# Sigmoid attention and a Swish feed-forward layer in one kernel: loading the first head group in halves, doubling the last value tile on chip, and reordering the products

## The chip, the cores and the metric

The kernel runs on one core of a Trainium2 chip. The metric is the device time of one execution in microseconds.

## What is computed

```python
# q, k, v: (8, 12, 448, 64): batch, heads, sequence, head size
scores = q @ k.T / sqrt(64) - log(448)
attn   = 1 / (1 + exp(-scores))             # a sigmoid, no row sums
x      = (attn @ v) -> (3584, 768)          # tokens x (heads * head size)
h      = x @ w_in                           # 768 x 2048
g      = h / (1 + exp(-beta * h))           # beta: one number per column
out    = g @ w_out                          # 2048 x 768, float32
```

## The kernel before, in words

Matmul operands are fp16, sums are fp32. The 12 heads of a batch are taken four at a time, a *group* g (24 groups, three per batch), and a group has two *slots* of two heads. `load_one` (L111) brings q and k of a group to the chip from POOL's queue, with a cast; `transpose` on DVE makes `qT` and `kT` (L183, L191, L195) in blocks of 32. `load_v` loads a batch's values. The 448 keys are three tiles of 128 and a last one of 64 keys; for odd slots the last tile is needed on partitions 64 to 127, so `load_v_last` loads it twice, with four loads (L144), for the lower and for the upper partitions.

`visit(g, jt)` computes the scores of one key tile for both slots on PE (L205) into two score tiles in PSUM, and ACT turns each into attention weights (L216). `attend(g)` multiplies them with the values on PE (L271) into two PSUM banks, and DVE copies these to `xT` (L280). `half_visit` does the same for half the queries (QH = 224) in batch 0's three groups, so that the first layer can begin early. `dense1` is a unit of the first layer: one column tile of 128, six matmuls (L289), a sigmoid on ACT (L297) and a product on DVE (L300) that writes `gt`.

The second layer takes most token tiles in pairs, by Strassen's scheme (`strassen`): seven products i of half size in place of eight, each in two parts of four matmuls (L401), with sums of `gt` on DVE (L390), copies from PSUM to `osb` on ACT for i = 1 and 2 (L423, L425), and additions on DVE (L420). The first three token tiles and the last are done plainly (`dense2`, L319, L332). `store` sends `osb` out from SP's queue (L454).

The order is written by hand (`manual_schedule`): each engine takes its instructions in program order. At the start PE runs matmuls without a use (`idle_units`, L513) while loads arrive. Later, a planner puts units of the list `fill` (first and second layer) between the visits: each visit adds to a budget (`spread`, then `rest`), and units with nominal costs (`M1_US`, `M1H_US`, `M2_US`) are taken until it is spent. Outside the score tiles, PSUM has four banks for everything. `bank` gives the one that has been out of use longest; a Strassen product that stays open is `held`. Ahead of an attend, the planner finishes units while more than one bank is held and the next unit opens one; the third entry that `second_layer` yields says so.

Of the kernel before, what the change touches and what calls it, by code (L numbers as in the profile page):

```python
# [8 lines left out]
FP32 = mybir.dt.float32  # L9
FP16 = mybir.dt.float16  # L10
# [3 lines left out]
def kernel(  # L14
# [10 lines left out]
    nc = tc.nc  # L25
# [26 lines left out]

    const = ctx.enter_context(tc.tile_pool(name="const", bufs=1))
    rawp = ctx.enter_context(tc.tile_pool(name="rawp", bufs=3))
    vp = ctx.enter_context(tc.tile_pool(name="vp", bufs=3))
    qTp = ctx.enter_context(tc.tile_pool(name="qTp", bufs=4))
    kTp = ctx.enter_context(tc.tile_pool(name="kTp", bufs=4))
    attnp = ctx.enter_context(tc.tile_pool(name="attnp", bufs=12))
    xTp = ctx.enter_context(tc.tile_pool(name="xTp", bufs=3))
    sump = ctx.enter_context(tc.tile_pool(name="sump", bufs=3))  # L60
    sigp = ctx.enter_context(tc.tile_pool(name="sigp", bufs=3))
    outp = ctx.enter_context(tc.tile_pool(name="outp", bufs=3))
    psum = {}
    used = {}
    held = {}
# [38 lines left out]
    raws = {}  # L104
    vs = {}

    def load_one(g: int, r: int, c0: int = 0, c1: int = NB):
        b, t = divmod(g, QPB)
        if g not in raws:
            raws[g] = rawp.tile([P, 2, NB, D], FP16, tag="raw", name="raw")  # L110
        nc.gpsimd.dma_start(  # L111
            out=raws[g][:, r, c0:c1].rearrange("p c d -> p (c d)"),
            in_=(q, k)[r][b, HQ * t : HQ * (t + 1)].rearrange("h (p c) d -> (h p) (c d)", c=NB)[
                :, c0 * D : c1 * D
            ],
        )

    def load_qk(g: int):
# [9 lines left out]
    def load_v(b: int):  # L128
        vs[b] = vp.tile([P, H, JF + 1, D], FP16, tag="v16", name="v16")
        rows = v[b].rearrange("h (p c) d -> p h (c d)", c=NB)  # L130
        for i in range(HQ):
            nc.gpsimd.dma_start(  # L132
                out=vs[b][i * BLK : (i + 1) * BLK, :, 0:JF].rearrange("p h j d -> p h (j d)"),
                in_=rows[:, :, JF * i * D : JF * (i + 1) * D],
            )
        if b > 0:
            load_v_last(b)

    def load_v_last(b: int):
        rows = v[b].rearrange("h (p c) d -> p h c d", c=NB)  # L140
        for base in (0, KL):
            for c in range(NF, NB):
                lo = base + (c - NF) * BLK
                nc.gpsimd.dma_start(  # L144
                    out=vs[b][lo : lo + BLK, :, JF], in_=rows[:, :, c]
                )

    WCH = 8
    WOUT = 2
# [24 lines left out]
    def in_order(b: int, t):  # L174
        t = t.rearrange("p c e -> p (c e)").bitcast(FP32)
        return t.rearrange("p (q c) -> p c q", c=NB) if b == B - 1 else t

    def transpose(g: int, r: int, c0: int = 0, c1: int = NB):
        raw = raws[g][:, r]
        if r == 0:  # L180
            if g not in qT:
                qT[g] = qTp.tile([P, NB * BLK, PAIR], FP16, tag="qT", name="qT")
            nc.vector.transpose(  # L183
                out=in_order(g // QPB, qT[g][:, c0 * BLK : c1 * BLK]),
                in_=raw[:, c0:c1].rearrange("p c d -> p (c d)").bitcast(FP32),
            )
            return
        kT[g] = kTp.tile([P, S, PAIR], FP16, tag="kT", name="kT")
        to = kT[g].rearrange("p k e -> p (k e)").bitcast(FP32)
        frm = raw.rearrange("p c d -> p (c d)").bitcast(FP32).rearrange("p (c f) -> p c f", c=NB)  # L190
        nc.vector.transpose(  # L191
            out=to[:, 0 : JF * P].rearrange("p (j i q) -> p i j q", j=JF, i=HQ),
            in_=frm[:, 0:NF].rearrange("p (i j) f -> p i j f", j=JF),
        )
        nc.vector.transpose(  # L195
            out=to[:, JF * P :], in_=frm[:, NF:].rearrange("p c f -> p (c f)")
        )

    def score_tile():
        return psum["sc"].tile([P, 2, 512], FP32, tag="sco", name="sco")  # L200
# [41 lines left out]
    def half_visit(g: int, c0: int, second: int):  # L242
        slots = (2 * g, 2 * g + 1)
        scos = [score_tile() for _ in slots]
        plan = [(s, jt, sco, jt * QH) for jt in (0, 1) for s, sco in zip(slots, scos)]
        widths = [S, S]
        if second:
            plan = [(s, 2, sco, 0) for s, sco in zip(slots, scos)]
            plan += [(s, JF, scos[0], QH) for s in slots]
            widths = [S, QH]  # L250
        for i in range(0, len(plan), 2):
            for e in range(PAIR):
                for s, jt, sco, u0 in plan[i : i + 2]:
                    for hh in range(2):
                        score(sco, u0, s, jt, hh, e, c0, QH)
        ats = {id(sco): weigh(sco, n) for sco, n in zip(scos, widths)}
        for s, jt, sco, u0 in plan:
            at_tiles[s, jt, c0] = ats[id(sco)][:, :, u0 : u0 + QH]
# [133 lines left out]
    def strassen(t: int, i: int, part: int):  # L392
# [29 lines left out]
        if i == 1:  # L422
            nc.scalar.copy(out=o2[:, L], in_=a)  # L423
        elif i == 2:
            nc.scalar.copy(out=o1[:, L], in_=m2)  # L425
            add(o1[:, R], r, o1[:, L])
            release((t, "s"))
        elif i == 3:
            add(o2[:, L], m2, o2[:, L])
            release((t, "b"))  # L430
        elif i == 4:
            add(o2[:, R], a, o2[:, L], ALU.subtract)
        elif i == 5:
            add(o2[:, R], r, o2[:, R])
            release((t, "r"))
            store(t + 1, 0, DM)
        elif i == 6:
            add(o1[:, L], a, o1[:, L], ALU.subtract)
            release((t, "a"))
            store(t, 0, DM)  # L440
# [19 lines left out]
    def second_layer(tiles):  # L460
        for t in tiles:
            if t < 3 or t == NT - 1:
                for half in range(2):
                    for part in range(N2):
                        yield M2_US / N2, lambda a=(t, half, part): dense2(*a), False
            elif t % 2:
                for i in range(NPROD):
                    for part in range(2):
                        yield M2_US / 4, lambda a=(t, i, part): strassen(*a), i in (2, 3)

    def filler_stream():
        for c0 in (0, QH):
# [24 lines left out]
    firsts = ctx.enter_context(ExitStack())  # L497
    share_psum(firsts, 3, 2)
    with tc.manual_schedule():
        load_one(0, 0, 0, NH)  # L500
        load_one(0, 1)
        nc.gpsimd.memset(nlogs, NEG_LOG_S)
        nc.gpsimd.memset(dummy, 0.0)
        nc.scalar.activation(out=dummy, in_=dummy, func=AF.Sigmoid, bias=0.0, scale=1.0)
# [7 lines left out]
            for _ in range(n):  # L512
                nc.tensor.matmul(idle, still[:, 0:P], still, start=True, stop=True)  # L513

        idle_units(13)
        for g in range(1, QPB):
            load_one(g, 0, 0, NH)
            load_one(g, 1)
        load_v(0)
        load_v_last(0)  # L520
        nc.sync.dma_start(out=beta_in[0:NDC], in_=moe_beta.rearrange("(c p) -> c p", p=P))
        for g in range(QPB):
            load_one(g, 0, NH, NB)
        for c in range(WCH):
            load_w_in(c)
        for g in range(QPB):
            transpose(g, 0, 0, NH)
            transpose(g, 1)

        for g in range(QPB):  # L530
            for second in range(2):
                half_visit(g, 0, second)
                if g == QPB - 1:
                    attend(0, 0, QH, (second,))
                if 2 * g + second < 2 * QPB - 1:
                    idle_units(4 if g < QPB - 1 else 2)
        for g in range(QPB):
            transpose(g, 0, NH, NB)
        attend(1, 0, QH, (0,))
        half_visit(0, QH, 0)  # L540
        attend(1, 0, QH, (1,))
        for i in range(P // BLK):
            part = slice(i * BLK, (i + 1) * BLK)
            nc.vector.transpose(out=beta_sb[part], in_=beta_in[:, part])
        attend(2, 0, QH)
        load_qk(3)
        load_w_out(0, 0)
        load_w_out(1, 0)
# [2 lines left out]
        load_qk(5)  # L551
        load_w_out(0, 1)
        load_w_out(1, 1)
        half_visit(0, QH, 1)

        firsts.close()
        share_psum(ctx, 2, 4)
# [5 lines left out]
                fill_units(1 + g)  # L563
        fill_units(2)
        attend(QPB - 1, QH, QH)
        transpose(QPB, 0)
        transpose(QPB, 1)
        fill_units(4)

        visits = [(QPB, jt, ()) for jt in range(JF + 1)]  # L570
        for g in range(QPB + 1, NQUAD, 2):
            visits += [(g, jt, ()) for jt in range(JF)] + [(g, JF, (g + 1,))]
            visits += [(g + 1, jt, ()) for jt in range(JF)]
        spread = [3 * M1H_US] * 2 + [M2_US, 6 * M1H_US] + [5 * M2_US / 7] * 7
        spread += [2.95] * (sum(g < 4 * QPB for g, _, _ in visits) - len(spread))

        total = sum(u[0] for u in fill[at_fill[0] :])
# [13 lines left out]
        for i, (g, jt, also) in enumerate(visits):  # L591
            if jt == 0:
                if g > QPB:

                    while len(held) > 1 and (len(held) > 2 or fill[at_fill[0]][3]):
                        spent += fill[at_fill[0]][0]
                        fill_units(1)
                    attend(g - 1, 0, S)
                if g + 2 < NQUAD:
                    if g + 2 not in raws:  # L600
                        load_qk(g + 2)
                if g + 1 < NQUAD and (g + 1) % QPB == 0:
                    load_v((g + 1) // QPB)
            visit(g, jt, also)
            if jt in (1, 2) and QPB < g < NQUAD - 1:
                transpose(g + 1, jt - 1)
            for name, part in adds.get(i, ()):
                weight_sum(name, part)
            budget += spread[i] if i < len(spread) else rest
            if (g, jt) == (QPB, JF):  # L610
                fill_units(3)
                spent += 3 * M1H_US
                transpose(g + 1, 0)
                transpose(g + 1, 1)
            goal = max(budget, spent + LEAST_US) if g > QPB + 2 else budget
# [38 lines left out]
```

## Time and profile before

| | us |
|---|---|
| median of 3 runs (391.8 to 392.15) | 391.82 |
| the profiled run | 391.83 |
| its span, first to last instruction | 390.1 |
| PE busy | 382.3 |
| ACT busy | 247.2 |
| DVE busy | 219.7 |
| POOL busy | 77.0 |

The profile records when each instruction ran, and what it had waited for. Engines: PE (matmuls; PEld is its weight loads), DVE (vector), ACT (activation functions), POOL and SP (here: issuing loads and stores). A busy PE is not a PE at its peak, because matmuls overlap each other; the distance from one start to the next says how fast they go. L271 is line 271 of the kernel before.

### The profile page before, as it was taken

Reading aid. Unit: us, or ns where it says so; the run is one execution under the profiler, and the core shown is the slowest. Engines: PE = TensorE matmul, PEld = TensorE weight load, DVE = VectorE, ACT = ScalarE, POOL = GpSimd, SP = SyncE. Lnnn points to the kernel's source line nnn. Section 1 sums busy time; section 2 is a strip of 40 time slices with the busy share of each in tenths; the row PEclk is TensorE's granted clock in tenths of the full one; section 3 lists DMA queues with packets and bytes.
Section 4 is the critical chain, followed back from the end, with each engine's and each line's share of the span. In section 5 each row is a group of like instructions: output and inputs, shape, how many; then the busy total and the mean of one; then the engine's idle time right before and its main releaser. Section 6 shows DMA issues by size and latency. Waiting matters only on the chain.

```text
span 390.1 us, 7403 instructions
## 1 busy us (share of the span) xinstructions
PE 382.3 (98%) x2991; PEld 191.4 (49%) x2991; DVE 219.7 (56%) x417; ACT 247.2 (63%) x341; POOL 77.0 (20%) x133
## 2 busy tenths in 40 slices
PE   8999999999999999999999999999999999999996
PEld 3468664444454444444454444544445444555563
DVE  2346364774655556555665556655675555555752
ACT  3987866688474796597465784567863677725200
POOL 7843353232110610150110510114100000000000
PEclk9999999999999999999999999999999999999999
DMA  8999999949252880547353581629113210030033
GB/s 120 158 187 202 185 179 203 208 86 95 49 105 63 125 92 4 119 69 71 49 117 81 83 81 28 126 50 163 27 22 82 52 31 2 1 82 0 2 81 121
DMA packets 48801, 35.08 MB, mean 90 GB/s; under 512 B 28272, under 2 KB 45184, under 8 KB 48768
## 3 DMA queue, kind: packets, MB, share of 16 engines
q0 software_dynamic: 43376, 23.60, 46.5%
q1 hardware_dynamic: 5392, 11.02, 10.5%
q8 instruction: 23, 0.38, 0.4%
q14 instruction: 10, 0.08, 0.1%
HBM read 47.19 MB, written 11.01 MB: 149 GB/s over the span
## 4 chain that ended last, share of the span: by engine, by line
PE 82%; DMA 9%; DVE 3%; POOL 2%; issue 2%; ACT 1%; SPq 0%; DVEq 0%; POOLq 0%
PE m_ps L289 37%; PE m_ps L401 25%; PE sco L205 9%; PE av_ps L271 8%; DMA w_out<-in_moe_w_out_dram 4%; PE m_ps L319 3%; DMA w_in<-in_moe_w_in_dram 2%; DMA out_dram<-osb 2%; DMA v<-in_v_dram 2%; POOL raw L111 1%; DVE osb L420 1%; DVE sum L390 1%; ACT osb L425 0%; POOL v L132 0%; SPq L454 0%
## 5 line engine op out<-in xcount | busy, mean ns | idle before, releaser
L216 ACT ACTIVATE attnT<-sco,nlogs 128x896 f16<-128x896 f32 (+1 forms) x171 | 160.4, 991 | 74.8 <-PE sco L205 74.1
L289 PE MATMUL m_ps<-xT,w_in 128*128 128x448 f16 (+1 forms) x864 | 154.3, 332 | 0.6 <-DMA w_in<-in_moe_w_in_dram 0.6
L300 DVE TENSOR_TENSOR gt<-m_ps,sg 128x448 f16<-128x448 f32 (+1 forms) x144 | 79.7, 571 | 87.2 <-ACT sg L297 87.1
L289 PEld LDWEIGHTS <-w_in 128*128 128x128 f16 x864 | 80.4, 98 | 71.3 <-issue 14.9
L297 ACT ACTIVATE sg<-m_ps,beta_sb 128x448 f32<-128x448 f32 (+1 forms) x144 | 82.1, 595 | 31.2 <-PE m_ps L289 29.8
L401 PEld LDWEIGHTS <-sum 128*128 128x128 f16 x480 | 45.1, 98 | 36.4 <-issue 7.9
L420 DVE TENSOR_TENSOR osb<-m_ps,osb 128x384 f32<-128x384 f32 x60 | 33.3, 555 | 38.4 <-ACT osb L425 19.5
L205 PE MATMUL sco<-qT,kT 32*128 32x448 f16 (+3 forms) x864 | 51.9, 340 | 0.5 <-DVE qT L183 0.2
L401 PE MATMUL m_ps<-w_T,sum 128*128 128x384 f16 x288 | 50.6, 327 | 0.0
L111 POOL DMA_DIRECT2D raw<-in_q_dram x27 | 14.9, 552 | 172.2 <-DVE kT L195 167.7
L271 PE MATMUL av_ps<-attnT,v 128*64 128x448 f16 (+3 forms) x432 | 43.3, 341 | 1.9 <-DVE osb L420 1.9
L280 DVE CAST xT<-av_ps 128x448 f16<-128x448 f32 (+1 forms) x54 | 28.7, 567 | 26.0 <-PE av_ps L271 26.0
L390 DVE TENSOR_TENSOR sum<-gt 128x1024 f16<-128x1024 f16 x60 | 39.0, 678 | 0.1
L401 PE MATMUL m_ps<-w_T,gt 128*128 128x384 f16 x192 | 33.9, 327 | 0.0
L401 PE MATMUL m_ps<-w_out,sum 128*128 128x384 f16 x192 | 33.7, 327 | 0.0
L271 PEld LDWEIGHTS <-v 128*64 128x64 f16 (+1 forms) x432 | 19.3, 108 | 27.3 <-issue 21.5
L205 PEld LDWEIGHTS <-kT 32*128 32x128 f16 (+1 forms) x864 | 13.5, 96 | 28.3 <-issue 26.0
L401 PEld LDWEIGHTS <-gt 128*128 128x128 f16 x192 | 18.1, 98 | 14.8 <-issue 3.1
L319 PE MATMUL m_ps<-w_out,gt 128*128 128x384 f16 (+2 forms) x128 | 22.5, 327 | 0.4 <-DMA w_out<-in_moe_w_out_dram 0.4
L132 POOL DMA_DIRECT2D v<-in_v_dram x32 | 19.8, 631 | 12.9 <-DMA w_out<-in_moe_w_out_dram 6.7
L144 POOL DMA_DIRECT2D v<-in_v_dram x32 | 19.5, 619 | 14.3 <-DMA w_out<-in_moe_w_out_dram 6.9
L183 DVE STREAM_TRANSPOSE qT<-raw 128x448 f32<-128x448 f32 (+1 forms) x27 | 16.4, 614 | 2.8 <-DMA raw<-in_q_dram 2.8
(23 smaller groups left out, 95.5 us busy)
## 6 DMA issues: line engine op xcount, KB each, us to landing
out_dram<-osb SPq DMA_DIRECT2D x98, 96.0 KB, 1.9
raw<-in_k_dram POOLq DMA_DIRECT2D x24, 224.0 KB, 4.9
raw<-in_q_dram POOLq DMA_DIRECT2D x21, 224.0 KB, 3.7
v<-in_v_dram POOLq DMA_DIRECT2D x32, 144.0 KB, 6.6
w_in<-in_moe_w_in_dram POOLq DMA_DIRECT2D x8, 384.0 KB, 11.0
w_out<-in_moe_w_out_dram POOLq DMA_DIRECT2D x4, 768.0 KB, 14.9
v<-in_v_dram POOLq DMA_DIRECT2D x32, 48.0 KB, 5.8
out_dram<-osb SPq DMA_DIRECT2D x2, 384.0 KB, 2.3
```

Source lines behind the costliest of these rows:

```text
L132: nc.gpsimd.dma_start(out=vs[b][i * BLK : (i + 1) * BLK, :, 0:JF].rearrange("p h j d -> p h (j d)"), in_=rows[:, :, JF * i * D : JF * (i + ...
L205: nc.tensor.matmul(sco[base : base + nk, hh, u0 : u0 + n], kT[g][lo : lo + BLK, jt * P : jt * P + nk, e], qT[g][lo : lo + BLK, c0 : c0 + n ...
L216: nc.scalar.activation(out=at[:, :, 0:n], in_=sco[:, :, 0:n], func=AF.Sigmoid, bias=nlogs[:, 0:1], scale=MSCALE,)
L271: nc.tensor.matmul(av[hh * D : (hh + 1) * D, 0:n], vs[b][base : base + nk, 2 * (s % NPAIR) + hh, jt], at[base : base + nk, hh, 0:n], start ...
L280: nc.vector.tensor_copy(out=xTs[b][:, s % NPAIR, c0 : c0 + n], in_=av[:, 0:n])
L289: nc.tensor.matmul(m1[:, 0:n], w_in16[:, hc, dc * P : (dc + 1) * P], xTs[b][:, hc, c0 : c0 + n], start=(hc == 0), stop=(hc == NHC - 1),)
L297: nc.scalar.activation(out=sg[:, 0:n], in_=m1[:, 0:n], func=AF.Sigmoid, bias=0.0, scale=beta_sb[:, dc : dc + 1])
L300: nc.vector.tensor_tensor(out=gt[:, dc, off : off + n], in0=m1[:, 0:n], in1=sg[:, 0:n], op=ALU.mult)
L319: nc.tensor.matmul(m2, gt[:, dc, cols(t)], w_out16[:, dc, lo:hi], start=(dc == 0), stop=(dc == NDC - 1),)
L390: nc.vector.tensor_tensor(out=sums[t, i], in0=x, in1=y, op=op)
L401: nc.tensor.matmul(m2, (x if op is None else sums[t, i])[:, dc], w[:, dc], start=first and dc == 0, stop=(dc == ND - 1), skip_group_check= ...
L420: nc.vector.tensor_tensor(out=out, in0=in0, in1=in1, op=op)
```

## The change

- The first group's q and k come in two pairs of heads, and transposes and scores of the first half visit are ordered by slot. The second half of its queries is loaded ahead of the values.
- The last value tile is loaded once, to the lower partitions. A DVE copy, `double_v_last`, brings it to the upper ones: for batch 0 after its first attend, for batch 1 after the key transposes of group 3, for the others at the third visit of their first group.
- The second query half's scores of group 0 move between the attends of the first half.
- Between `attend(2)` and the planner, five units surround the transposes of group 3 in place of four; the first entries of `spread` change.
- The copy of product i = 2 moves from ACT to DVE; part 0 of product 4 counts as a unit that comes ahead of an attend.
- There are two value buffers for three, four output buffers for three, and 10 idle matmuls at the start for 13.

```diff
-    vp = ctx.enter_context(tc.tile_pool(name="vp", bufs=3))
+    vp = ctx.enter_context(tc.tile_pool(name="vp", bufs=2))
-    outp = ctx.enter_context(tc.tile_pool(name="outp", bufs=3))
+    outp = ctx.enter_context(tc.tile_pool(name="outp", bufs=4))
...
-        if b > 0:
-            load_v_last(b)
-
-    def load_v_last(b: int):
         rows = v[b].rearrange("h (p c) d -> p h c d", c=NB)
-        for base in (0, KL):
-            for c in range(NF, NB):
-                lo = base + (c - NF) * BLK
-                nc.gpsimd.dma_start(
-                    out=vs[b][lo : lo + BLK, :, JF], in_=rows[:, :, c]
-                )
+        for c in range(NF, NB):
+            lo = (c - NF) * BLK
+            nc.gpsimd.dma_start(out=vs[b][lo : lo + BLK, :, JF], in_=rows[:, :, c])
+
+    def double_v_last(b: int):
+        nc.vector.tensor_copy(out=vs[b][KL:P, :, JF], in_=vs[b][0:KL, :, JF])
...
+        if (g, c0) == (0, 0):
+            plan.sort(key=lambda x: x[0])
+            side = 1
...
         elif i == 2:
-            nc.scalar.copy(out=o1[:, L], in_=m2)
+            nc.vector.tensor_copy(out=o1[:, L], in_=m2)
...
-                        yield M2_US / 4, lambda a=(t, i, part): strassen(*a), i in (2, 3)
+                        yield M2_US / 4, lambda a=(t, i, part): strassen(*a), i in (2, 3) or (i, part) == (4, 0)
...
-        load_one(0, 0, 0, NH)
-        load_one(0, 1)
+        for h in (0, 2):
+            load_one(0, 0, 0, NH, h, h + 2)
+            load_one(0, 1, 0, NB, h, h + 2)
...
-        idle_units(13)
+        idle_units(10)
         for g in range(1, QPB):
             load_one(g, 0, 0, NH)
             load_one(g, 1)
+        load_one(0, 0, NH, NB)
         load_v(0)
-        load_v_last(0)
         nc.sync.dma_start(out=beta_in[0:NDC], in_=moe_beta.rearrange("(c p) -> c p", p=P))
-        for g in range(QPB):
+        for g in range(1, QPB):
             load_one(g, 0, NH, NB)
...
                 half_visit(g, 0, second)
-                if g == QPB - 1:
-                    attend(0, 0, QH, (second,))
                 if 2 * g + second < 2 * QPB - 1:
                     idle_units(4 if g < QPB - 1 else 2)
-        for g in range(QPB):
-            transpose(g, 0, NH, NB)
+        attend(0, 0, QH, (0,))
+        double_v_last(0)
+        half_visit(0, QH, 0)
+        attend(0, 0, QH, (1,))
+        for g in range(1, QPB):
+            transpose_q(g, NH, NB)
         attend(1, 0, QH, (0,))
-        half_visit(0, QH, 0)
         attend(1, 0, QH, (1,))
...
-        attend(2, 0, QH)
+        attend(2, 0, QH, (0,))
+        half_visit(0, QH, 1)
+        attend(2, 0, QH, (1,))
         load_qk(3)
         load_w_out(0, 0)
         load_w_out(1, 0)
         load_v(1)
         load_qk(4)
         load_qk(5)
         load_w_out(0, 1)
         load_w_out(1, 1)
-        half_visit(0, QH, 1)
...
         attend(QPB - 1, QH, QH)
+        fill_units(1)
         transpose(QPB, 0)
+        fill_units(2)
         transpose(QPB, 1)
-        fill_units(4)
+        double_v_last(1)
+        fill_units(2)
...
-        spread = [3 * M1H_US] * 2 + [M2_US, 6 * M1H_US] + [5 * M2_US / 7] * 7
+        spread = [4 * M1H_US, M1H_US + M2_US, 6 * M1H_US, 3 * M2_US / 4]
+        spread += [17 * M2_US / 4 / 7] * 7
...
             if jt in (1, 2) and QPB < g < NQUAD - 1:
                 transpose(g + 1, jt - 1)
+            if jt == 2 and g % QPB == 0 and g > QPB:
+                double_v_last(g // QPB)
...
             if (g, jt) == (QPB, JF):
                 fill_units(3)
-                spent += 3 * M1H_US
+                spent += 3 * M2_US / N2
```

More of the change, by code (lines that the diff above doesn't have):

```diff
@@ L105, with load_one @@
     vs = {}
-    def load_one(g: int, r: int, c0: int = 0, c1: int = NB):
+    def load_one(g: int, r: int, c0: int = 0, c1: int = NB, h0: int = 0, h1: int = HQ):
         b, t = divmod(g, QPB)
@@ L111, in load_one @@
         nc.gpsimd.dma_start(
[L112 to L115, printed above, removed]
+            out=raws[g][h0 * BLK : h1 * BLK, r, c0:c1].rearrange("p c d -> p (c d)"),
+            in_=(q, k)[r][b, HQ * t + h0 : HQ * t + h1].rearrange(
+                "h (p c) d -> (h p) (c d)", c=NB
+            )[:, c0 * D : c1 * D],
         )
@@ L176, in in_order, with transpose_q, transpose_k, transpose @@
         return t.rearrange("p (q c) -> p c q", c=NB) if b == B - 1 else t
-    def transpose(g: int, r: int, c0: int = 0, c1: int = NB):
-        raw = raws[g][:, r]
-        if r == 0:
[L181 to L197, printed above, removed]
+    def transpose_q(g: int, c0: int = 0, c1: int = NB, rows=slice(0, P)):
+        if g not in qT:
+            qT[g] = qTp.tile([P, NB * BLK, PAIR], FP16, tag="qT", name="qT")
+        nc.vector.transpose(
+            out=in_order(g // QPB, qT[g][rows, c0 * BLK : c1 * BLK]),
+            in_=raws[g][rows, 0, c0:c1].rearrange("p c d -> p (c d)").bitcast(FP32),
+        )
+    def transpose_k(g: int, last: int, rows=slice(0, P)):
+        if g not in kT:
+            kT[g] = kTp.tile([P, S, PAIR], FP16, tag="kT", name="kT")
+        to = kT[g][rows].rearrange("p k e -> p (k e)").bitcast(FP32)
+        frm = raws[g][rows, 1].rearrange("p c d -> p (c d)").bitcast(FP32)
+        frm = frm.rearrange("p (c f) -> p c f", c=NB)
+        if last:
+            to, frm = to[:, JF * P :], frm[:, NF:].rearrange("p c f -> p (c f)")
+        else:
+            to = to[:, 0 : JF * P].rearrange("p (j i q) -> p i j q", j=JF, i=HQ)
+            frm = frm[:, 0:NF].rearrange("p (i j) f -> p i j f", j=JF)
+        nc.vector.transpose(out=to, in_=frm)
+    def transpose(g: int, r: int):
+        if r == 0:
+            transpose_q(g)
+        else:
+            transpose_k(g, 0)
+            transpose_k(g, 1)
     def score_tile():
@@ L245, in half_visit @@
         plan = [(s, jt, sco, jt * QH) for jt in (0, 1) for s, sco in zip(slots, scos)]
-        widths = [S, S]
+        widths, side = [S, S], 2
+        if (g, c0) == (0, 0):
+            plan.sort(key=lambda x: x[0])
+            side = 1
         if second:
@@ L249, in half_visit @@
             plan += [(s, JF, scos[0], QH) for s in slots]
-            widths = [S, QH]
-        for i in range(0, len(plan), 2):
+            widths, side = [S, QH], 2
+        for i in range(0, len(plan), side):
             for e in range(PAIR):
-                for s, jt, sco, u0 in plan[i : i + 2]:
+                for s, jt, sco, u0 in plan[i : i + side]:
                     for hh in range(2):
@@ L525 @@
             load_w_in(c)
-        for g in range(QPB):
-            transpose(g, 0, 0, NH)
-            transpose(g, 1)
+        halves = (slice(0, KL), slice(KL, P))
+        for rows in halves:
+            transpose_q(0, 0, NH, rows)
+            transpose_k(0, 0, rows)
+        for rows in halves:
+            transpose_k(0, 1, rows)
+        for g in range(1, QPB):
+            transpose_q(g, 0, NH)
+            transpose_k(g, 0)
+            transpose_k(g, 1)
+        transpose_q(0, NH, NB)
         for g in range(QPB):
@@ L532 @@
                 half_visit(g, 0, second)
-                if g == QPB - 1:
-                    attend(0, 0, QH, (second,))
                 if 2 * g + second < 2 * QPB - 1:
                     idle_units(4 if g < QPB - 1 else 2)
-        for g in range(QPB):
-            transpose(g, 0, NH, NB)
+        attend(0, 0, QH, (0,))
+        double_v_last(0)
+        half_visit(0, QH, 0)
+        attend(0, 0, QH, (1,))
+        for g in range(1, QPB):
+            transpose_q(g, NH, NB)
         attend(1, 0, QH, (0,))
-        half_visit(0, QH, 0)
         attend(1, 0, QH, (1,))
```

## The prediction

> **What bounds the kernel now.** I read the page first, then the chain of waits in order of time, then PE's own timeline, and last the landing times of single loads.
>
> ```profile
> span 390.1 us, 7403 instructions
> PE 382.3 (98%) x2991; PEld 191.4 (49%) x2991; DVE 219.7 (56%) x417; ACT 247.2 (63%) x341; POOL 77.0 (20%) x133
> ```
>
> The profiled run took 391.83 us, 1.7 us outside its span, and the median of the runs is 391.82, so I sum in the span and add 1.7. A PE that is busy for 98% leaves gains only where its matmuls start late. The chain says where that is, from the start to 63 us:
>
> ```profile
> 6.52 6.91 DMA v<-in_v_dram
> ...
> 13.71 0.82 POOL w_in L153
> 14.53 7.82 DMA w_in<-in_moe_w_in_dram
> ...
> 49.76 13.65 DMA w_out<-in_moe_w_out_dram
> ```
>
> Up to there one stream of loads, issued by POOL in program order, sets the end; after 63.45 us the chain is nearly all PE. In PE's timeline I compared each group of matmuls with its undisturbed twin, start to start. From 41.94 us on it loses: 0.22 and 0.46 us in the scores of `visit(3,1)` and `visit(3,2)` (0.73 and 0.97 us against 0.51), 0.63 us at the w_out load that lands at 63.4, and at six attends, those that follow Strassen products, 0.43 us five times (2.00 against 1.57) and 0.88 us once, together 3.03. That makes 4.34 us.
>
> **The part that decides.** The change loads the last value tile once and lets DVE copy it to the upper partitions. For batch 1 that copy, `double_v_last(1)`, stands on DVE right after the key transposes of group 3. When does DVE get there, and when has its input landed?
>
> ```profile
> 38.57 0.20 DVE L195 STREAM_TRANSPOSE kT<-raw 128x64 f32<-128x64 f32 x1
> 38.70 0.73 DVE L300 TENSOR_TENSOR gt<-m_ps,sg 128x224 f16<-128x224 f32 x2
> 39.59 0.12 PEld L205 LDWEIGHTS <-kT 32*128 32x128 f16 x8 [0.18 <-DVE gt L300]
> ```
>
> ```profile
> L144 POOL DMA_DIRECT2D v<-in_v_dram x1: 609/609/609, 37.1 to 37.1; - x1
> ...
> DMA to landing us min/median/max: 11.5/11.5/11.5
> ```
>
> DVE ends those transposes at 38.8 us. The two loads that the copy reads are the first two of L144 for batch 1; they are issued at 36.53 and 37.13 and land 11.8 and 11.5 us later, at 48.3 and 48.6, behind two w_out loads of 768 KB. The order of POOL's issues there is unchanged. Before, only `attend(3)` at 52.25 us needed them, so the wait was hidden; now DVE stands at its copy for some 9 us. Queued behind it are the products gt (L300) of the next first-layer units. Each frees one of four PSUM banks, so PE can run four more units and the unit after them, column tile 7 of batch 0's second half, stops it.
>
> Does DVE really let ready work stand?
>
> ```profile
> 103.08 0.48 ACT L425 COPY osb<-m_ps 128x384 f32<-128x384 f32 x1 [0.82 <-PE m_ps L401]
> 103.59 0.56 DVE L420 TENSOR_TENSOR osb<-m_ps,osb 128x384 f32<-128x384 f32 x1 [1.35 <-ACT osb L425]
> 104.06 0.68 DVE L390 TENSOR_TENSOR sum<-gt 128x1024 f16<-128x1024 f16 x1
> 104.27 0.76 PE L271 MATMUL av_ps<-attnT,v 128*64 128x448 f16 x6
> 104.66 0.55 DVE L420 TENSOR_TENSOR osb<-m_ps,osb 128x384 f32<-128x384 f32 x1
> 105.26 1.07 PE L271 MATMUL av_ps<-attnT,v 128*64 128x448 f16 x10 [0.24 <-DVE osb L420]
> ```
>
> Yes: the sum at 104.06 reads only gt, complete long before, and its buffer was free when PE ended the third product at about 103.0; it still ran behind the add that DVE idled 1.35 us for. The Trainium skill, "TensorE: Matmul & The Clock Gate", Part 1, says the same, that VectorE's queue is strict FIFO; if it were not, rival A would be the result.
>
> *When PE goes on.* Loads land earlier than before by two terms. Two 48 KB loads of v(0) fall out; the last two of L144 there landed at 15.0 and 15.3, the one before at 14.5: 0.8 us. And the stream had a dip:
>
> ```profile
> 11.00:14.00 3.00, 3.00 (x38) 1.19 (x38) 0.00 (x0) 3.00 (x4) 2.07 (x5) 1.00 1.88 173
> 14.00:17.00 3.00, 3.00 (x54) 1.38 (x42) 0.60 (x2) 2.95 (x4) 3.00 (x5) 1.00 1.00 124
> ```
>
> At 124 instead of 173 GB/s (last column) 3 us lose 0.85. POOL issued the first w_in load only at 13.71, after a wait for a landing of v; now smaller loads stand ahead of it and it should go out some 2 us sooner. I take 0.7 (0 to 0.85). Landing: 48.6 − 0.8 − 0.7 = 47.1 (46.9 to 47.8). Then the copy, 768 fp16 elements on 64 partitions, a shape not in the trace: the sum of 1024 takes 0.68 us, the smallest transposes 0.20; I take 0.4, nearer to the middle because a copy reads one operand. Then gt, 0.39 us (L300 at 128x224), and 0.1 of waits: PE resumes at 48.0 us (47.5 to 49).
>
> *What is then left of PE's work.* Before, the same work (tiles 0 to 6, `visit(3,0)`) is done at 41.94 us, with 348.1 us still to go. This does not depend on the edits ahead of it: group 0 by head pairs, the earlier query halves, `half_visit(0,QH,·)` among the attends, 10 idle matmuls for 13 all end in the same wait, so I cost them at nothing. Were the wait gone, they would be worth at most the 1.5 us by which w_in lands earlier, because PE already waits for w_in at 22.4.
>
> *Clock.* PE stands idle from about 40.5 (41.94 less up to 1.5) to 48.0, for 7.5 us. What a PE does after standing still, the start of the span shows:
>
> ```profile
> 1.19 5.54 PE L513 MATMUL idle_ps<-still 128*128 128x512 f16 x13 [1.19 <-DVE still L507]
> ...
> 7.41 1.04 PE L513 MATMUL idle_ps<-still 128*128 128x512 f16 x4
> ```
>
> Until 6.28 us matmuls of 512 columns start every 0.427 us; those from 7.41 every 0.216. So 12 matmuls lose 12 × 0.211 = 2.5 us. No row shows a long idle time later in the kernel; the bounds are 0 and 2.5, and I take 2.5 because the start is the only row with a PE that has stood still. (PEclk reads 9 there too, so that line will not show it.) The same page and part of the Trainium skill states that the array's clock halves after an idle window of about 3.4 us and comes back after a busy one, with windows that run freely: 1.7 to 3.4 us lost as an estimate from it, and a sum of 397.1 to 398.8 instead of 397.9.
>
> **The rest, gains and losses after 48 us.** The 4.34 us listed above: the w_out wait (0.63) goes because PE comes later; `visit(3,1)` and `visit(3,2)` get four and five units ahead of them instead of three (0.68 gone). The attend stalls: each waits for the bank that the fourth product's add frees. The copy of the third product on DVE takes about what ACT's took (0.56 against 0.48), so the add ends as before, but `(i, part) == (4, 0)` puts four matmuls, 0.66 us, ahead of the attend: more than 0.43. The 0.88 case came from ACT's copy at 117.1, behind two sigmoids, after a store at 113.94; DVE's copy and the fourth output buffer remove both. I take all 3.03 (0 to 3.03). Left: 348.1 − 4.3 = 343.8.
>
> A loss is added: with `17 * M2_US / 4 / 7` per visit, by the planner's own sums, only two second-layer units stand between `visit(4,0)` and `(4,1)`, `(4,2)` and `(4,3)`, `(5,0)` and `(5,1)`. A visit's scores need both score tiles free, and ACT ends 2.51 us after a visit starts (39.60 to 40.21 + 1.90 = 42.11). Two units give 0.51 + 2 × 0.687 = 1.88: 3 × 0.63 = 1.9 us (0 to 1.9). Before, three units made it fit.
>
> At nothing: the other six or seven copies (about 0.4 us each; DVE is 56% busy, and each comes a whole group or more after its loads were queued), value buffers 2 for 3 (batch 2's predecessor is read last before 37 us), 16 fewer POOL issues of 0.62.
>
> Sum: 48.0 + 343.8 + 1.9 + 2.5 = 396.2, and 1.7 outside: **397.9 us**, 1.6% slower.
>
> **Rivals.** *A, no wait, faster:* the copy's loads land before DVE gets there, or DVE passes it. Then PE is 1.5 us earlier at 41.94: 40.4 + 343.8 + 1.9 + 1.7 = 387.8 us. For it speaks only that attends and start are sound; against it, landing must move from 47.1 to under 38. It breaks even where PE resumes at 44.4 (at 41.9 with a slow clock). *B, the wait without a slow clock:* 395.4. For it: no mid-kernel row; against it: the start. *C, the wait, but attends stall as before* because DVE, with more to do, frees the bank later: 400.9. Against it: 0.66 of cover for 0.43. The change does what it says in all of them.
>
> **Numbers.** Forecast 0.58, B 0.17, A 0.10, C 0.10, a mixture between B and no change 0.05. The time is the forecast's. The range, 394.0 to 400.4, takes in B and most of C, with the bounds of the resume time and of the tight visits; it leaves out A and the edges. A measurement tells 0.2%, 0.8 us, from no change: slower 0.88, same 0.02, faster 0.10.
>
> **What would show it.** A DVE copy of v that idles about 9 us for DMA v and ends near 47.5; PE idle before a L289 matmul from about 40.5 to 48; slow spacing for some 5 us after it; attends after Strassen products at 1.57 us; three score groups of visits 4 and 5 at 1.1. I am wrong if v's tail lands before 40 us, or if PE finds other work in that gap.

## The result and the profile after

| | before | changed |
|---|---|---|
| median, us | 391.99 | 399.03 |
| lowest to highest | 391.8 to 393.02 | 398.7 to 399.97 |
| ratio | | 1.0173 (1.0152 to 1.0195) |
| span of the profiled run | 390.1 | 397.0 |
| PE busy | 382.3 | 383.4 |
| DVE, ACT, POOL busy | 219.7, 247.2, 77.0 | 231.1, 242.3, 68.3 |

Slower by 1.7%, where 1.6% was forecast (397.9 us, range 394.0 to 400.4). The page of the changed kernel has a row of the granted clock in 40 slices of the span, in tenths of full speed:

```profile
PEclk9999889999999999999999999999999999999999
```

The two 8s, slices 5 and 6, cover about 40 to 60 us. From the timeline there, lines of DVE and PE:

```profile
40.74 0.69 DVE L193 STREAM_TRANSPOSE kT<-raw 128x384 f32<-128x384 f32 x2
...
41.87 1.32 PE L296 MATMUL m_ps<-xT,w_in 128*128 128x224 f16 x12
...
47.95 0.44 DVE L142 COPY v<-v 64x768 f16<-64x768 f16 x1 [6.51 <-DMA v<-in_v_dram]
48.42 1.36 DVE L307 TENSOR_TENSOR gt<-m_ps,sg 128x224 f16<-128x224 f32 x4
48.87 2.40 PE L296 MATMUL m_ps<-xT,w_in 128*128 128x224 f16 x12 [5.67 <-DVE gt L307]
```

DVE ends group 3's key transposes at 41.4 us and stands for 6.5 us at the copy, until the last load of batch 1's v, its tail, has landed (issued at 36.59, 11.3 us to landing, 47.9). PE runs two more units and then, ahead of column tile 7 of batch 0's second half (unit 7 from here on), stands idle for 5.67 us, for the product that is queued behind the copy. The 12 matmuls after it take 2.33 us start to start, where 12 of the same shape at 25.6 us took 1.26. That the clock has fallen shows in the stretches (the third value from the right is the granted clock):

```profile
40.00:48.00 8.00, 2.90 (x32) 2.10 (x30) 1.49 (x6) 3.54 (x6) 2.82 (x5) 0.90 1.49 196
48.00:58.00 10.00, 9.13 (x67) 5.83 (x67) 3.48 (x9) 5.11 (x8) 2.21 (x4) 0.74 1.26 205
```

Further on, one of the three score groups that come too early for ACT (PE's timeline), and a Strassen attend that waits no longer (all engines):

```profile
66.49 0.37 PE L208 MATMUL sco<-qT,kT 32*128 32x448 f16 x2
67.14 0.57 PE L208 MATMUL sco<-qT,kT 32*128 32x448 f16 x6 [0.28 <-ACT attnT L219]
```

```profile
113.08 0.56 DVE L432 COPY osb<-m_ps 128x384 f32<-128x384 f32 x1 [0.83 <-PE m_ps L408]
...
114.74 0.55 DVE L427 TENSOR_TENSOR osb<-m_ps,osb 128x384 f32<-128x384 f32 x1
...
114.92 1.64 PE L278 MATMUL av_ps<-attnT,v 128*64 128x448 f16 x16
```

The add that frees the second bank ends at 115.3, and the attend's 16 matmuls run in one piece.

### The profile page after: what moved, and what is told of

It is laid out like the page before. It is cut to its first block, busy times and chain, and to the rows that moved or that the text cites. A ratio compares the mean times of both kernels' runs of the same rounds, so it can differ in the third digit from the quotient of the medians.

```text
span 397.0 us, 7374 instructions
## 1 busy us (share of the span) xinstructions
PE 383.4 (97%) x2988; PEld 192.2 (48%) x2988; DVE 231.1 (58%) x440; ACT 242.3 (61%) x329; POOL 68.3 (17%) x119
## 4 chain that ended last, share of the span: by engine, by line
PE 85%; DMA 10%; ACT 2%; POOL 1%; issue 1%; DVE 0%; DVEq 0%; POOLq 0%
PE m_ps L296 35%; PE m_ps L408 28%; PE sco L208 10%; PE av_ps L278 8%; DMA raw<-in_k_dram 5%; PE m_ps L326 4%; DMA v<-in_v_dram 3%; DMA w_in<-in_moe_w_in_dram 2%; ACT attnT L219 1%; POOL raw L111 1%; POOL w_in L149 0%; DVE gt L307 0%; DVE v L142 0%; ACT sg L304 0%; DVE osb L339 0%
## 5 line engine op out<-in xcount | busy, mean ns | idle before, releaser
L296 PE MATMUL m_ps<-xT,w_in 128*128 128x448 f16 (+1 forms) x864 | 156.5, 335 | 6.1 <-DVE gt L307 6.0
L296 PEld LDWEIGHTS <-w_in 128*128 128x128 f16 x864 | 81.4, 99 | 77.6 <-issue 21.7
L208 PE MATMUL sco<-qT,kT 32*128 32x448 f16 (+3 forms) x864 | 53.6, 342 | 3.1 <-DVE kT L193 1.8
L408 PE MATMUL m_ps<-w_T,sum 128*128 128x384 f16 x288 | 51.6, 327 | 0.0
L278 PE MATMUL av_ps<-attnT,v 128*64 128x448 f16 (+3 forms) x432 | 42.2, 340 | 0.1
L408 PEld LDWEIGHTS <-gt 128*128 128x128 f16 x192 | 18.1, 98 | 14.7 <-issue 3.1
L132 POOL DMA_DIRECT2D v<-in_v_dram x32 | 19.8, 636 | 5.4 <-DMA w_in<-in_moe_w_in_dram 5.3
L193 DVE STREAM_TRANSPOSE kT<-raw 128x384 f32<-128x384 f32 (+3 forms) x50 | 17.6, 387 | 4.1 <-DMA raw<-in_k_dram 4.0
L177 DVE STREAM_TRANSPOSE qT<-raw 128x448 f32<-128x448 f32 (+2 forms) x28 | 17.0, 608 | 2.5 <-DMA raw<-in_q_dram 2.5
```

The lines of the kernel that those rows point to most:

```text
L132: nc.gpsimd.dma_start(out=vs[b][i * BLK : (i + 1) * BLK, :, 0:JF].rearrange("p h j d -> p h (j d)"), in_=rows[:, :, JF * i * D : JF * (i + ...
L208: nc.tensor.matmul(sco[base : base + nk, hh, u0 : u0 + n], kT[g][lo : lo + BLK, jt * P : jt * P + nk, e], qT[g][lo : lo + BLK, c0 : c0 + n ...
L278: nc.tensor.matmul(av[hh * D : (hh + 1) * D, 0:n], vs[b][base : base + nk, 2 * (s % NPAIR) + hh, jt], at[base : base + nk, hh, 0:n], start ...
L296: nc.tensor.matmul(m1[:, 0:n], w_in16[:, hc, dc * P : (dc + 1) * P], xTs[b][:, hc, c0 : c0 + n], start=(hc == 0), stop=(hc == NHC - 1),)
L408: nc.tensor.matmul(m2, (x if op is None else sums[t, i])[:, dc], w[:, dc], start=first and dc == 0, stop=(dc == ND - 1), skip_group_check= ...
```

## The experiments

Theory: DVE's wait at `double_v_last(1)` sets when PE goes on, and a slow clock follows; the edits of the Strassen part are worth 3 us. Rival: the wait only hides another limit, the load stream or the new order, so that without it the time would stay.

**1. The copy late.** Ahead of `attend(3)`, the first that reads it.

```diff
-        double_v_last(1)
         fill_units(2)
...
                 transpose(g + 1, 0)
                 transpose(g + 1, 1)
+                double_v_last(1)
```

> The changed kernel with one line moved: the DVE copy of batch 1's last value tile comes after the transposes of group 4, just ahead of attend(3), in place of right behind the key transposes of group 3. Theory (DVE's wait at that copy costs the time): the 5.7 us that PE stands idle at 43.2 us and the 1.9 to 2.0 us of slow matmuls after it both go, span 397.0 - 7.6 = 389.4 us, time about 391.2 us, ratio to the kernel before about 0.998. Rival (the copy's wait only hides another limit, the load stream or the new order of units): at least half of the 7 us stay, 395 us or more.

Measured: 392.29 us, ratio 0.9996 (0.9981 to 1.0011), profiled span 389.7. PE's timeline has no wait at unit 7, which begins 1.2 us into this line:

```profile
42.30 2.38 PE L296 MATMUL m_ps<-xT,w_in 128*128 128x224 f16 x23
```

The 1.7% are gone with one line moved; the rival falls. The median is 1.1 us over the forecast because the executions differ: those with a mean granted clock of 0.999 or more took 390.96 to 391.46 (one 393.56), those with 0.994 to 0.996 took 392.28 to 392.65. The profiled execution had 0.999, so no trace here shows where the others lost their clock; runs 3 and 10 point to the start. The one of 393.56, at a clock of 1.0, stays unexplained.

**2. PE busy in the wait.**

```diff
         for _ in range(n):
+            if at_fill[0] == 23:
+                warm = score_tile()
+                for _ in range(24):
+                    nc.tensor.matmul(warm[:, 0], still[:, 0:P], still, start=True, stop=True)
             fill[at_fill[0]][2]()
```

> The changed kernel with 24 matmuls without a use (512 columns, 0.216 us each, 5.2 us in all) put on PE just ahead of the first-layer unit that waits, into a score tile that is free then. The wait stays, PE is busy in it. Theory (PE runs slow after standing idle): unit 7 still starts at about 48.9 us, but the 12 matmuls after it start every 0.1 us and not every 0.19, and the time falls by 1.9 to 2.0 us to about 397.1 us. Rival (the slow stretch is the backlog of DVE and ACT): the stretch after 48.9 stays as it is, 399 us.

Measured: 397.69 us, ratio 1.0137 (1.012 to 1.0154). PE's timeline:

```profile
42.90 5.34 PE L503 MATMUL sco<-still 128*128 128x512 f16 x24
49.94 1.31 PE L296 MATMUL m_ps<-xT,w_in 128*128 128x224 f16 x12 [1.69 <-DVE gt L307]
```

The 12 matmuls now take 1.24 us start to start, with the same backlog on DVE and ACT: the slow stretch was the clock. Unit 7 starts 1.1 us later than in the changed kernel because v's tail landed at 48.8 in this execution; by the medians the filling is worth 1.3 us, less than the 1.9 to 2.0 expected.

**3. Late copy, units dealt out evenly.** On top of run 1:

```diff
-        spread += [17 * M2_US / 4 / 7] * 7
+        spread += [n * M2_US / 4 for n in (3, 3, 3, 1, 3, 3, 1)]
```

> The late copy, and the 17 second-layer units among the visits of groups 4 and 5 dealt out as 3, 3, 3, 1, 3, 3, 1. Theory (two units between two visits are 0.64 us too few for ACT's two sigmoids): 1.9 us less than the late copy alone, perhaps 0.2 to 0.3 given back at the attend of group 5: 389.3 to 389.6 us, ratio about 0.993. Rival (ACT is late there for another reason, or the wait moves to the attends): 391 us, as the late copy alone.

Measured: 391.05 us, ratio 0.997 (0.9951 to 0.9989), executions from 389.18 to 392.12. All scores of groups 4 and 5 are back at 0.51 to 0.53 us, and the attend of group 5 gives 0.41 back. The three executions of 389.18 to 389.69, all with a mean clock of 1.0, agree with the forecast. Six with 0.99 to 0.996 took 390.99 to 392.1, and one took 392.12 at 0.999, which stays unexplained. The profiled one, of 392.1, lost at the start, where it ran at half clock:

```profile
9.00:14.00 5.00, 5.00 (x40) 1.48 (x39) 2.14 (x6) 2.03 (x4) 3.19 (x6) 0.50 1.40 173
```

**4. Group 0 loaded whole** in the changed kernel.

```diff
-        for h in (0, 2):
-            load_one(0, 0, 0, NH, h, h + 2)
-            load_one(0, 1, 0, NB, h, h + 2)
+        load_one(0, 0, 0, NH)
+        load_one(0, 1)
```

> The changed kernel with group 0's q and k loaded whole again, in two loads of 128 partitions and not four of 64. In the changed kernel k of group 1 lands at 10.02 us and not 8.52, and the whole stream keeps that lag. Theory (the halves slow the stream, and the stream sets when PE goes on): the last value tile of batch 1 lands about 1.2 us earlier, 46.7 and not 47.9, PE goes on that much earlier, time about 397.8 us. Rival (the lag comes from the other order of loads): it lands at 47.9 as before, 399 us.

Measured: 397.26 us, ratio 1.0126 (1.0099 to 1.0152). DVE's and PE's timelines:

```profile
46.62 0.35 DVE L142 COPY v<-v 64x768 f16<-64x768 f16 x1 [3.52 <-DMA v<-in_v_dram]
```

```profile
47.45 1.31 PE L296 MATMUL m_ps<-xT,w_in 128*128 128x224 f16 x12 [2.59 <-DVE gt L307]
```

v's tail lands at 46.6, as forecast: 1.26 us earlier than in the changed kernel. Profiled executions differ among themselves by nearly as much, but the two sets stay apart: with the halves the tail lands at 47.9 (the change), 48.5 (runs 1 and 3), 48.8 (run 2) and 48.7 (run 10), with group 0 whole at 46.6 and at 46.8 (run 9). In this execution PE came late from a slow start (first layer from 23.67 us, not 22.0; clock 0.66 between 9 and 14 us), stood idle for 2.59 us only, and the clock stayed at 1.00; that one took 395.44, the others 397.1 to 397.9.

**5. The copies alone, in the kernel before.** One load of the last value tile and `double_v_last` at the places of the change, batch 1's ahead of the four units.

```diff
         transpose(QPB, 0)
         transpose(QPB, 1)
+        double_v_last(1)
         fill_units(4)
```

> The kernel before with one part of the change alone: the last value tile loaded once and copied by DVE, batch 1's copy right behind the key transposes of group 3. Theory (DVE's wait there): four units stand behind the copy and use up the banks, so PE stops one visit earlier, at about 40.1 us, until v's tail has landed (47.5 to 47.9) plus 0.9 for copy and product: 48.4 to 48.8 us, then slow matmuls for 2 us. From there 349.9 us of the old work less the 1.3 us of early waits that the delay hides: span about 399 us, time 400.5 us, ratio 1.022. Rival (the loss in the changed kernel comes from the other edits of its start and order): no more than 394 us.

Measured: 400.46 us, ratio 1.0211 (1.0195 to 1.0228), span 399.0. All engines:

```profile
47.49 0.35 DVE L146 COPY v<-v 64x768 f16<-64x768 f16 x1 [9.66 <-DMA v<-in_v_dram]
47.87 1.36 DVE L300 TENSOR_TENSOR gt<-m_ps,sg 128x224 f16<-128x224 f32 x4
48.31 2.02 PE L289 MATMUL m_ps<-xT,w_in 128*128 128x224 f16 x10 [9.08 <-DVE gt L300]
```

This part alone is slower than the whole change. With four units behind the copy PE stops three units earlier than in the change (120 first-layer matmuls are done, not 138) and stands for 9.08 us.

**6. The planner's entry alone, in the kernel before.**

```diff
-                        yield M2_US / 4, lambda a=(t, i, part): strassen(*a), i in (2, 3)
+                        yield M2_US / 4, lambda a=(t, i, part): strassen(*a), i in (2, 3) or (i, part) == (4, 0)
```

> The kernel before, and only the planner's entry for part 0 of product 4 changed. Theory (0.66 us of matmuls ahead of the attend cover the bank's 0.43): five attends lose their 0.43 us and the sixth keeps 0.2 of 0.88: about 2.8 us less, 389.2 us, ratio 0.993. Rival (the bank comes free later when its turn comes later): 392 us.

Measured: 389.35 us, ratio 0.9936 (0.992 to 0.9952). Five attends are at 1.57 us, start to start, and the sixth keeps 0.24 of its loss. One of the five, which took 2.00 before, in PE's timeline:

```profile
105.11 1.64 PE L271 MATMUL av_ps<-attnT,v 128*64 128x448 f16 x16
```

**7. The copy on DVE and the buffers alone, in the kernel before.**

```diff
-            nc.scalar.copy(out=o1[:, L], in_=m2)
+            nc.vector.tensor_copy(out=o1[:, L], in_=m2)
```

> The kernel before, and only the copy of product 2 moved to DVE, with four output buffers and two value buffers. Theory: the copy does not end earlier where ACT is free, so five attends keep their 0.43 us, and only the attend with 0.88 us, where ACT's copy stood behind two sigmoids, falls to 0.43: 0.4 to 0.5 us less, 391.5 us, ratio 0.999. Rival (the chain from ACT to DVE is what delays the bank): all six fall, 389 us.

Measured: 391.94 us, ratio 0.9995 (0.998 to 1.0009): no difference. The attend with 0.88 falls, as expected, but to 0.51, and the other five rise from 0.43 to 0.51: the copy's 0.56 us on DVE are 0.08 more than ACT's 0.48, and the bank's add ends that much later. One gains 0.37, five lose 0.40. The second part of the first of them, whose wait was 0.24 before:

```profile
105.41 1.07 PE L271 MATMUL av_ps<-attnT,v 128*64 128x448 f16 x10 [0.32 <-DVE osb L420]
```

**8. The best of both.** The kernel before with its own start; one load of the last value tile, the late copy, both Strassen edits, the even units, five units around group 3's transposes as in the change.

> The kernel before with its own start, and of the change what I take to be good: the last value tile loaded once, batch 1's copy late (ahead of attend(3)), both edits of the Strassen part, and the units dealt out evenly between the visits of groups 4 and 5. Theory: 3.0 us at the attends, 0.7 at visits of group 3, 0.6 at the w_out load, up to 0.8 at the start because w_in lands earlier, 0.4 back at the attend of group 5: about 387.3 us, ratio 0.988. Rival (the start of the changed kernel is as good): no better than the late copy with even units, 390 to 391 us.

Measured: 387.92 us, ratio 0.9892 (0.9878 to 0.9907), span 385.9: faster than both kernels, 0.6 us over the forecast.

**9 and 10. Which edit of the start is slow?** The late copy with even units (run 3), with 13 idle matmuls; in run 9 with group 0 whole, in run 10 in halves.

```diff
-        idle_units(10)
+        idle_units(13)
```

> The late copy with even units, with 13 idle matmuls at the start again and group 0's q and k loaded whole: what is left of the change's start is the earlier load of group 0's second query half and the order of scores and attends. Theory (halved loads and a clock that falls in some executions make the start of the changed kernel slow): the clock stays at 1.0 in every execution, w_in lands 1.2 us earlier, time 388.5 us, within 0.3% of the version with the old start (387.9). Rival (the order is what is slow): 390 us or more.

> As the run beside it, with group 0's loads in halves as the change has them: only the idle matmuls, 13 for 10, set it apart from the late copy with even units. Theory (the fall of the clock at the start comes from PE standing still too long after 10 of them): the executions with a clock of 0.99 go, all at 1.0, time 389.3 to 389.7 us; the halved loads still cost about 1 us against the run beside it. Rival (the idle matmuls have no part in it): a spread from 389.2 to 392.1 as before.

Measured: 389.19 us, ratio 0.9927 (0.9913 to 0.994), and 389.60 us, ratio 0.9939 (0.9927 to 0.9952); the intervals overlap. In run 10 all five executions lie between 389.33 and 389.77 with a clock of 0.999 to 1.0, so the spread of run 3 came from 10 idle matmuls in place of 13. Run 9 lies between its theory (388.5) and its rival (390 or more), 0.7 us above the first: with the loads whole and the clock up, 1.3 us against run 8 remain. Its trace points to the order. The first w_in load lands at 18.1 us in run 9 and 18.2 in run 8, but PE begins the first layer at 22.09 and 20.18. In run 9, ACT's timeline:

```profile
21.65 1.53 ACT L219 ACTIVATE attnT<-sco,nlogs 128x896 f16<-128x896 f32 x2 [1.51 <-PE sco L208]
```

ACT has worked off all scores by 20.1 and then waits, because `half_visit(0, QH, 1)` comes behind four half attends that PE takes first, from 18.14 to 20.84. No run moved that one call alone, so this cause is read from the trace and not tested. The halves delay the first w_in load to 20.5 us in run 10, but PE is not there before 22.26 anyway.

## Why the prediction was right, and where it was not

Its mechanism held: the wait, the idle PE and the slow clock after it. The sizes came out partly by luck. PE goes on 0.87 us later than forecast and six units cost 0.5 that the sum put at nothing; the slow clock cost 0.55 less and hides part of that. The terms of the sum, with what the changed kernel's profile has:

| term | forecast | measured |
|---|---|---|
| v's tail lands | 47.1 | 47.86 |
| copy | 0.4 | 0.44 |
| PE goes on | 48.0 | 48.87 |
| PE idle | 7.5 | 5.67 |
| slow clock | 2.5 | 1.95 |
| three tight visits | 1.9 | 0.64 + 0.66 + 0.64 = 1.94 |
| attends | 3.03 saved | 3.03 saved |
| work from there, at full pace | 343.8 | 343.7, what is left of the span |
| six units after `visit(3,2)` | 0 | 0.5 |
| span | 396.2 | 397.0 |

With the forecast's own 343.8 the measured terms give 48.87 + 343.8 + 1.94 + 1.95 + 0.5 = 397.1, against a span of 397.0. PE's idle time isn't in that sum: it ends where PE goes on. The other copies of the value tile, put at nothing, waited for no load: the profile lists one such wait of DVE at L142, the 6.5 us.

- *The wait.* Right, by both proofs: taken away (run 1) the loss goes, put alone into the kernel before (run 5) it appears, and larger. The forecast that edits ahead of the wait don't count for the end held for PE's work: PE reached its last unit before the wait 2.7 us later than forecast (43.2, not 40.5), and only the idle time shrank.
- *The landing.* The two terms for an earlier stream had the right sign and came out larger together: 48.6 to 46.6 with group 0 whole (run 4), 2.0 us for 1.5. Wrong was to cost the halved loads at nothing: they come ahead of the wait but take part in setting its end, by 1.26 us in that pair of traces.
- *The clock.* Shown by run 2. The size: 1.11 in the first 12 matmuls (2.33 against 1.22, two thirds of what 18 took at 40.11 us before), 0.36 in a group of scores, 0.48 in the next six. The estimate from the page "TensorE: Matmul & The Clock Gate" of the Trainium skill, Part 1, was 1.7 to 3.4, and the trace agrees: 1.95 us were lost. It also fits that 5.67 us of idle time lowered the clock and 2.59 us in run 4 did not. That the row PEclk would not show it was wrong: the row has two 8s, and the stretches above 0.90 and 0.74.
- *The Strassen part.* The sum was right, its division not. The planner's entry has nearly all of it (run 6); the copy on DVE and the buffers give 0.2 beside it and nothing alone (run 7). "Takes about what ACT's took" left out 0.08 us on a chain that five attends wait for.
- *Tight visits.* Right in place and size; run 3 took them away.
- *The range.* It was said to take in most of rival C, the attends that stall as before, but C's own figure of 400.9 lies above its upper end, 400.4. C didn't occur.
- *The six units* wait for sigmoids that stand behind the attention weights on ACT. I had moved them ahead of a visit without asking what ACT does then. The chain of the changed kernel shows it:

```profile
56.44 1.84 PE m_ps L296 x18
58.28 0.44 ACT sg L304
...
59.19 1.31 PE m_ps L296 x12
```

- *Rival A*, no wait, was given 387.8 us. Run 1 is that case and took 391.0 to 391.5 at full clock (but for the one of 393.56): unit 7 starts there at 43.5 us, not 40.4, and the six units cost 0.5. "Worth at most 1.5" had the wrong sign: in these profiled executions the edits ahead of the wait are worth minus 1.6 us (43.5 against 41.94).

## What to carry to other kernels

An instruction that waits for a load blocks everything behind it on its engine: before replacing a load by an on-chip copy, compare when the engine reaches the copy with when the load lands, and put the copy just ahead of its first reader. Once such a wait is found, sum the end from it, not from the start: what lies ahead then matters only where it moves the wait's end. A few matmuls of other work between the freeing of a bank and its next use can be worth more than a faster path to freeing it.

## What the runs showed of the hardware beyond expectation

- Four loads of half the partitions in place of two delayed the loads behind them: v's tail by 1.26 us and the first w_in load by 1.5 us (run 4 against the change), that load by 2.4 us in run 10 against run 9 (20.5 and 18.1). POOL takes 0.54 to 0.66 us for these issues of either size, so each of the first four carries half as much in the same time; whether that pace is the whole cause was not tried.
- PE's clock fell to 0.50 between 9 and 14 us in one execution of run 3 and stayed at 1.00 there in one of run 1, with the same start, 10 idle matmuls. The longest idle time of PE between its first matmul and that stretch was 1.58 us in run 3 and 1.41 in run 1, both shorter than the 2.59 us that did no harm in run 4, so the length of a single gap doesn't tell when the clock falls; what does stays open. With 13, no execution of run 9 or 10 had a mean under 0.999.
